# Moving the activation loads of the second half into buffers that the first half no longer needs

## The chip, the cores and the metric

The kernel runs on one core of one Trainium2 chip. The metric is device time in microseconds (us), median of several executions. "Span" is the length of one profiled execution; it is about 2 us shorter than the timed execution.

Short names: PE is the matrix engine (TensorE), PEld its loading of the operand that stays in place, DVE the vector engine, ACT the scalar engine, POOL the GpSimd engine. SPq is the queue of the sync engine, which issues nearly all loads. `ring` is a set of 20 buffers that all weights pass through, and the halo is the few columns of keys and values that a chunk takes over from the chunk before it. The granted clock is the share of full speed that TensorE was given. L552 means line 552 of that kernel's own source, so the same statement has different line numbers in different kernels.

## The reference, cut to what matters

```python
# S = 2048 rows, D = 1024, Df = 3584, 32 heads of 32, bf16
g = sigmoid((x * gate_w).sum(-1, keepdims=True))
# attention: every position looks at 8 positions, 2 apart, up to 14 back
qkv = x @ wqkv ; attn = softmax(q . k[pos - 2*w] * scale) ; a = (attn . v[pos - 2*w]) @ wo
# gated MLP
b = (gelu(x @ w_gate) * (x @ w_up)) @ w_down
out = g * a + (1 - g) * b
```

## The kernel before

The sequence is cut into four chunks of 512 rows. PE works in this order: transposes, QKV of chunks 0 and 1, gate/up pass of chunks 0 and 1, `down` of chunk 0, **QKV of chunks 2 and 3 together**, `down` of chunk 1, gate/up pass of chunks 2 and 3, `down` of chunks 2 and 3. The attention arithmetic of the chunks runs on DVE beside all this.

The larger products use seven half-size products in place of eight. This needs *forms*: sums and differences of quarters of the weights and of the activations. Most weight forms of `down` and gate/up are computed once and stored. The weight forms of the QKV product of chunks 2 and 3 are made by DVE just before use (L552, `ring<-ring`, 0.42 us each), and four activation forms (L449 to L454, `tf<-xr`, 1.2 us each) too.

Each engine runs its instructions in a fixed order. The Python program chooses this order at build time with a list scheduler: it keeps a modelled clock for every engine and always emits the operation that could start first by its own model.

```python
class Weave:
    def _emit(self, op, t):
        if op.eng in ("SP", "POOL"):            # a load: bytes at a modelled rate, issue cost
            nbytes, issue = op.cost
            self.clk[op.eng] = t + issue
            self.pipe = max(self.pipe, t) + nbytes / self.RATE
            op.end = self.pipe + 2.2
        else:
            self.clk[op.eng] = t + cost
        ...                                     # and is chained behind the engine's last instruction
    def run(self, streams):
        ...
                t = None if op is None else self._start(op)     # after all deps, by the model
                if t is not None and (best is None or t + s[0] < best[0]):
                    best = (t + s[0], t, s, op)
```

The parts that the change touches:

```python
xr = persist.tile([P, 4, KH, SC], BF16)                   # activations of two chunks
kT = [persist.tile([P, NT, HALO + SC], BF16, ...) for i in range(2)]   # keys: one per chunk parity
vT = [persist.tile([P, NT, HALO + SC], BF16, ...) for i in range(2)]   # values

def load_x(c, deps):                                      # 8 transposing loads of 128 KB a chunk
    for kt in range(KT):
        yield Op("SP", (P * SC * 2, 1.6), lambda kt=kt: nc.sync.dma_start_transpose(
            out=xT(c, kt), in_=x[c * SC:(c + 1) * SC, kt * P:(kt + 1) * P]), deps, key=("x", c, kt))

def loads():                                              # order of the load queue
    ...
    # among the weights of down(chunk 0): the 16 loads of chunks 2 and 3
    yield from load_down(c0, [o for c in (c0 + 2, c0 + 3) for o in load_x(c, [("ffn", sup)])])
    for which in range(3):
        yield from load_qkv(c0 + 2, which, ...)           # then the QKV weights
```

`xr` is read until the end of the first gate/up pass, so chunks 2 and 3 cannot be loaded earlier than that.

## Time and profile before

| what | value | view |
|---|---|---|
| time | 740.24 us (739.6 to 740.36, 3 runs) | timed runs |
| span | 738.2 us | page |
| PE busy | 723.9 us, 98% | page, part 1 |
| PE waiting for weight forms | 7.7 us in 3 pieces | waits |
| granted PE clock just after | 0.50, then 0.89 | windows |

The page's part 1 (busy time, share of the span, instructions):

```profile
PE 723.9 (98%) x3397; PEld 355.7 (48%) x3397; DVE 631.1 (85%) x935; ACT 312.7 (42%) x530; POOL 72.0 (10%) x128
```

Whom PE waited for, in the kernel before (us in total, times, longest):

```profile
PE ps L585 <- DVE ring L552: 7.7, 3, 4.2
PE ps L274 <- DVE hT L272: 1.2, 1, 1.2
PE ps L1191 <- DMA hT<-in_A_x_dram: 0.9, 1, 0.9
PE ps L1096 <- DMA ring<-in_A_wo_dram: 0.6, 2, 0.4
```

PE is the limit nearly everywhere. The only large wait is for L552, the QKV weight forms. The table of windows (each line: stretch in us, its length, then busy us of PE, PEld, DVE, ACT, POOL with instruction counts, granted clock, DMA share, GB/s) shows where it lies:

```profile
300.00:318.00 18.00, 17.35 (x79) 7.48 (x77) 17.86 (x22) 0.69 (x1) 2.69 (x5) 1.00 1.12 354
322.00:329.00 7.00, 0.81 (x2) 0.23 (x2) 7.00 (x13) 0.00 (x0) 0.00 (x0) 0.79 0.34 128
329.00:332.00 3.00, 2.55 (x7) 0.95 (x8) 3.00 (x11) 0.59 (x1) 0.00 (x0) 0.50 0.00 0
332.00:336.00 4.00, 4.00 (x18) 2.27 (x17) 3.30 (x10) 2.35 (x4) 0.00 (x0) 0.89 0.00 0
```

PE works 0.81 of 7 us at 322 to 329 us, and the clock falls to half within this stretch. Before that, DMA is saturated (share 1.12). The timeline of the load queue (start, duration, what was issued) shows the transposing loads standing in front of the QKV weights:

```profile
299.95 4.20 SPq L307 DMA_TRANSPOSE xr<-in_A_x_dram  x3
304.25 3.39 SPq L357 DMA_DIRECT2D ring<-dforms  x7
308.64 1.16 SPq L307 DMA_TRANSPOSE xr<-in_A_x_dram  x1
309.89 35.21 SPq L302 DMA_DIRECT2D ring<-in_A_wqkv_dram  x16
```

One more view belongs here, although the prediction made too little of it: DVE's timeline (start, duration, instruction, output<-input; an idle time before an instruction would stand in brackets at the end).

```profile
316.50 2.47 DVE L771 TENSOR_TENSOR xbuf<-xbuf 128x2048 bf16<-128x2048 bf16 x2
319.01 2.31 DVE L828 STREAM_TRANSPOSE xbuf<-xbuf 128x2048 bf16<-128x2048 bf16 x1
321.24 1.18 DVE L449 TENSOR_TENSOR tf<-xr 128x2048 bf16<-128x2048 bf16 x1
322.35 0.41 DVE L552 TENSOR_TENSOR ring<-ring 128x512 bf16<-128x512 bf16 x1
322.68 1.22 DVE L451 TENSOR_TENSOR tf<-xr,tf 128x2048 bf16<-128x2048 bf16 x1
...
328.98 4.78 DVE L552 TENSOR_TENSOR ring<-ring 128x512 bf16<-128x512 bf16 x14
```

No line has a bracket. The form at 322.35 was preceded by attention work of chunk 1 (L771, L828), with no idle time. So DVE was not waiting for weights when it reached the form. It was late by its own order. The landings say the same: the two loads that the first form needs were issued at 309.9 and 310.5 us and landed 4.9 and 5.1 us later, by 315.6 us, and the form came 6.8 us after that.

### The profile page before, as it was taken

How to read it: one execution, taken by the hardware profiler on the slowest of the kernel's cores; microseconds unless marked ns; L12 is line 12 of the kernel's file. 1: busy time of each engine (PE TensorE's matmuls, PEld its weight loads, DVE VectorE, ACT ScalarE, POOL GpSimd, SP SyncE). 2: the span in 40 equal slices, each digit the busy share in tenths (PEclk: the TensorE clock that was granted, in tenths of full speed). 3: DMA queues.
4: the chain of work that ended last, by engine and by line, in shares of the span. 5: the costliest groups of instructions: out<-in, count | busy, mean ns of one | idle time of the engine just before them, and what ended most of it. 6: DMA issues, size and time to landing. Idle time of an engine off the chain costs nothing.

```text
span 738.2 us, 9955 instructions
## 1 busy us (share of the span) xinstructions
PE 723.9 (98%) x3397; PEld 355.7 (48%) x3397; DVE 631.1 (85%) x935; ACT 312.7 (42%) x530; POOL 72.0 (10%) x128
## 2 busy tenths in 40 slices
PE   8999999999999999959999999999999999999997
PEld 5666644444444444425665444444444444444443
DVE  2689899999999999997999999989999999896300
ACT  2333455558555542015444122585558554310110
POOL 2235322121111000000000001000000000001000
PEclk9999999999999999989999999999999999999999
DMA  9999955555646469950235999746464545889993
GB/s 304 332 331 361 377 190 177 165 175 168 200 143 207 156 193 327 321 223 28 86 115 175 314 312 317 245 134 181 128 176 134 166 142 158 284 302 335 323 303 105
DMA packets 150435, 162.68 MB, mean 220 GB/s; under 512 B 22896, under 2 KB 110960, under 8 KB 150384
## 3 DMA queue, kind: packets, MB, share of 16 engines
q1 hardware_dynamic: 141552, 134.25, 59.0%
q0 software_dynamic: 8544, 27.27, 10.3%
q8 instruction: 26, 0.43, 0.2%
q10 hardware_dynamic: 288, 0.52, 0.2%
q14 instruction: 25, 0.20, 0.1%
HBM read 129.50 MB, written 28.31 MB: 214 GB/s over the span
## 4 chain that ended last, share of the span: by engine, by line
PE 95%; DMA 3%; DVE 1%; issue 0%; ACT 0%; DVEq 0%
PE ps L952 46%; PE ps L1096 28%; PE ps L469 11%; PE ps L585 10%; DMA ring<-in_A_wo_dram 1%; DMA ring<-oforms 1%; DMA ring<-in_A_wqkv_dram 1%; DMA hT<-in_A_x_dram 0%; PE ps L1191 0%; DVE zt L699 0%; DVE tf L451 0%; DVE tf L449 0%; PE ps L693 0%; DVE ring L552 0%; ACT ost L1131 0%
## 5 line engine op out<-in xcount | busy, mean ns | idle before, releaser
L952 PEld LDWEIGHTS <-ring 128*128 128x128 bf16 x1568 | 153.2, 98 | 185.0 <-issue 0.4
L952 PE MATMUL ps<-xr,ring 128*128 128x512 bf16 x896 | 212.3, 379 | 0.0
L952 PE MATMUL ps<-tf,ring 128*128 128x512 bf16 x672 | 164.0, 379 | 0.0
L1096 PE MATMUL ps<-ring,hT 128*128 128x512 bf16 x708 | 160.7, 379 | 0.0
L1096 PEld LDWEIGHTS <-hT 128*128 128x128 bf16 x708 | 69.2, 98 | 83.4
L765 DVE TENSOR_TENSOR xbuf<-qo,kT 128x2048 bf16<-128x2048 bf16 x64 | 77.5, 1218 | 2.1 <-ACT kT L491 2.1
L904 DVE TENSOR_TENSOR xbuf<-xbuf,vT 128x2048 bf16<-128x2048 bf16 x64 | 77.4, 1218 | 0.1
L771 DVE TENSOR_TENSOR xbuf<-xbuf 128x2048 bf16<-128x2048 bf16 x56 | 68.2, 1218 | 0.1
L585 PEld LDWEIGHTS <-ring 128*128 128x128 bf16 x336 | 44.0, 131 | 38.6 <-DVE ring L552 10.0
L1131 ACT ACTIVATE ost<-ps,omg 128x512 bf16<-128x512 f32 x16 | 11.0, 688 | 113.4 <-PE ps L1096 110.2
L469 PE MATMUL ps<-xr,ring 128*128 128x512 bf16 x256 | 56.1, 381 | 0.1
L981 ACT COPY ps<-ps 128x512 f32<-128x512 f32 x56 | 32.0, 571 | 55.0 <-PE ps L952 54.8
L1123 POOL DMA_DIRECT2D out_dram<-ost x24 | 13.0, 540 | 433.0 <-ACT ost L1131 339.2
L1024 ACT ACTIVATE gl<-ps 128x512 bf16<-128x512 f32 x56 | 33.5, 598 | 51.3 <-PE ps L952 50.9
L1096 PE MATMUL ps<-ring,qo 128*128 128x512 bf16 x192 | 49.6, 379 | 0.6 <-DMA ring<-in_A_wo_dram 0.6
L996 DVE TENSOR_TENSOR hT<-hT,gl 128x1024 bf16<-128x1024 bf16 x56 | 38.4, 686 | 8.6 <-ACT hT L993 7.6
L469 PEld LDWEIGHTS <-ring 128*128 128x128 bf16 x256 | 36.6, 144 | 19.0 <-issue 0.9
L585 PE MATMUL ps<-xr,ring 128*128 128x512 bf16 x192 | 43.5, 379 | 0.0
L1036 DVE TENSOR_TENSOR u<-ps,u 128x512 f32<-128x512 f32 x56 | 38.4, 686 | 5.3 <-PE ps L952 4.2
L585 PE MATMUL ps<-tf,ring 128*128 128x512 bf16 x144 | 35.1, 394 | 7.7 <-DVE ring L552 7.7
L912 DVE TENSOR_TENSOR xbuf<-xbuf 128x1024 bf16<-128x1024 bf16 x64 | 42.0, 686 | 0.6
L438 POOL DMA_DIRECT2D fforms<-ring x56 | 30.5, 544 | 119.3 <-DVE ring L430 115.4
(106 smaller groups left out, 728.1 us busy)
## 6 DMA issues: line engine op xcount, KB each, us to landing
ring<-dforms SPq DMA_DIRECT2D x112, 256.0 KB, 4.7
ring<-in_B_w_down_dram SPq DMA_DIRECT2D x84, 256.0 KB, 3.9
ring<-in_B_w_gate_dram SPq DMA_DIRECT2D x56, 256.0 KB, 4.8
fforms<-ring POOLq DMA_DIRECT2D x56, 256.0 KB, 4.4
ring<-fforms SPq DMA_DIRECT2D x56, 256.0 KB, 3.9
ring<-in_B_w_up_dram SPq DMA_DIRECT2D x42, 256.0 KB, 3.9
ring<-in_A_wqkv_dram SPq DMA_DIRECT2D x40, 256.0 KB, 5.7
ring<-oforms SPq DMA_DIRECT2D x32, 256.0 KB, 5.4
```

What stands on the lines that cost most here:

```text
L469: nc.tensor.matmul(banks[bk][:], lhsT=lhsT, rhs=xT(c, kt), start=(kt == 0), stop=(kt == KT - 1))
L585: nc.tensor.matmul(banks[bk][:], lhsT=lhsT, rhs=rhs[:, kt, :], start=(start and kt == 0), stop=(kt == KH - 1), skip_group_check=True)
L765: V(out=w3(box[t]), in0=q_b, in1=k_w, op=ALU.mult)
L771: V(out=w3(box[0]), in0=w3(box[0]), in1=w3(box[t]), op=ALU.add)
L904: return dve(tt(n), taking(("p", t), lambda: V(out=w3(box["p", t]), in0=w3(box["ab"]), in1=v_w, op=ALU.mult)), [("qkv", c, 2, t), abo] + ( ...
L912: V(out=s4(t)[:, t % 2], in0=w3(box["p", t])[:, 0:4], in1=w3(box["p", t])[:, 4:8], op=ALU.add)
L952: nc.tensor.matmul(banks[bk][:], lhsT=wv[:, k, fl * P:(fl + 1) * P], rhs=rhs[:, k, :], start=(start and k == 0), stop=(k == KH - 1), skip_ ...
L981: ev[f, "seed"] = act(0.5, lambda f=f: nc.scalar.copy(out=banks[Bk[f]][:], in_=banks[A[f]][:]), [o, fr] if fr else [o])
L996: yield dve(tt(2 * SC), lambda f=f: nc.vector.tensor_tensor(out=hT[:, :, f, :], in0=hT[:, :, f, :], in1=gl[f][:].rearrange("p (j s) -> p j ...
L1024: nc.scalar.activation(out=gl[f][:, SC:2 * SC], in_=banks[A[f]][:], func=ACT.Gelu_apprx_tanh)
L1036: e = dve(tt(SC, True), lambda f=f: nc.vector.tensor_tensor(out=u2[f][:], in0=banks[Dk[f]][:], in1=u2[f][:], op=ALU.add), [o, ev[f, "u2"]])
L1096: nc.tensor.matmul(banks[bk][:], lhsT=l, rhs=wv[:, i, :], start=(start and k == 0), stop=(q == last and i == 1), skip_group_check=True)
```

## The change

The intent: load the activations of chunks 2 and 3 during the first gate/up pass, where DMA has room, instead of while `down` of chunk 0 loads its weights. Room is found by letting them live in the key and value buffers of chunk 0, which are dead after chunk 0's attention, and by rotating six buffers among keys, values and activations. Chunk 3's values have no place yet when they are computed, so they wait in dead rows of `h` and are moved by DMA. Some smaller savings of memory come along: the halo is 14 instead of 16 columns, one gate buffer serves for three, and the gate's exponential is issued next to the softmax's. The core of the diff (cut):

```diff
-    xr = persist.tile([P, 4, KH, SC], BF16)
-    kT = [persist.tile([P, NT, HALO + SC], BF16, name=f"kT{i}") for i in range(2)]
-    vT = [persist.tile([P, NT, HALO + SC], BF16, name=f"vT{i}") for i in range(2)]
+    lend = [persist.tile([P, NT, HALO + SC], BF16, name=f"lend{i}") for i in range(6)]
+    xs = [z[:]... for z in lend[0:4]]                      # x of chunks 0..3
+    kT = [lend[2], lend[4], lend[0], lend[4]]
+    vT = [lend[3], lend[5], lend[1], lend[5]]
+    XB = 9
     def load_x(c, deps):
+        deps = deps + ([[("acct", 1)], [("att", 0)]][c - 2] if c > 1 else [])
@@ loads
         for b in range(2, NBLK):
             yield from load_block(0, b)
+            if b >= XB:                                    # after gate/up blocks 9, 10, 11, 12
+                for c, k0 in ((2, 0), (2, 4), (3, 0), (3, 4))[b - XB:b - XB + 1]:
+                    yield from list(load_x(c, []))[k0:k0 + 4]
-                yield from load_down(c0, [o for c in (c0 + 2, c0 + 3) for o in load_x(c, [("ffn", sup)])])
+                yield from load_down(c0)
@@ x_forms, of chunks 2 and 3
-            free = [("pr", c0 - 2, 2, 1), ("S2", c0 - 2, 0), ("S2", c0 - 2, 1)] if sup else []
+            free = [("ffn", sup - 1)] if sup else []
@@ qkv_pair: values of chunk 3
+            if odd and which == 2:
+                return v_tmp(t), ("v3", t), []             # dead h rows; v_move() copies them later
... (halo 14, scratch of down(0) in lend[0:2], merged exponentials, zq instead of zc and og)
```

More of the change, by code (lines that the diff above doesn't have):

```diff
@@ L18 @@
 DIL = 2
-HALO = 16
+HALO = 14
 SC = 512
@@ L192 @@
     qo = [persist.tile([P, NT, SC], BF16, name=f"qo{i}") for i in range(2)]
-    kT = [persist.tile([P, NT, HALO + SC], BF16, name=f"kT{i}") for i in range(2)]
-    vT = [persist.tile([P, NT, HALO + SC], BF16, name=f"vT{i}") for i in range(2)]
+    lend = [persist.tile([P, NT, HALO + SC], BF16, name=f"lend{i}") for i in range(6)]
+    xs = [z[:].rearrange("p t s -> p (t s)")[:, 0:NT * SC].rearrange("p (t s) -> p t s", s=SC) for z in lend[0:4]]
+    kT = [lend[2], lend[4], lend[0], lend[4]]
+    vT = [lend[3], lend[5], lend[1], lend[5]]
     NG = 20
@@ L207, in xT, with xq @@
     def xT(c, kt):
-        return xr[:, 2 * (c % 2) + kt // KH, kt % KH, :]
+        return xs[c][:, kt, :]
+    def xq(c, hi):
+        return xs[c][:, KH * hi:KH * (hi + 1), :]
     def hflat(j, f0, n):
@@ L339, with load_down @@
     SEQ = [("A11", "B11"), ("A12", "B21"), ("S1", "T1"), ("S2", "T2"), ("S3", "T3"), ("S4", "B22"), ("A22", "T4")]
-    def load_down(c, extra=(), first=()):
-        extra = list(extra)
+    def load_down(c, first=()):
         for m, (_, name) in enumerate(SEQ):
@@ L359, in load_down @@
                     ([("stored", "o" if o else "d")] if name[0] == "T" else []) + [("w", 0, NBLK - 1, 3)] + list(first))
-            if m >= 1:
-                yield from extra[:3]
-                extra = extra[3:]
     def loads():
@@ L389, in loads @@
                                         [("wq", c0 + 2, which - 1, 3, KH - 1)] if which else [])
-                yield from load_down(c0 + 1, (), [("wq", c0 + 2, 2, 3, KH - 1)])
+                yield from load_down(c0 + 1, [("wq", c0 + 2, 2, 3, KH - 1)])
                 for b in range(NBLK):
@@ L442, in x_forms @@
     def x_forms():
-        b12, b22, b11, b21 = xr[:, 0], xr[:, 1], xr[:, 2], xr[:, 3]
         t = tt(KH * SC)
@@ L447, in x_forms @@
             dx = [("x", c0 + 1, kt) for kt in range(KT)]
-            free = [("pr", c0 - 2, 2, 1), ("S2", c0 - 2, 0), ("S2", c0 - 2, 1)] if sup else []
-            t1 = dve(t, lambda: V(out=tf[:, 0], in0=b12, in1=b11, op=ALU.subtract), dx + free, lag=1.0, key=("xf", sup, 1))
+            b12, b22, b11, b21 = xq(c0, 0), xq(c0, 1), xq(c0 + 1, 0), xq(c0 + 1, 1)
+            free = [("ffn", sup - 1)] if sup else []
+            t1 = dve(t, lambda b12=b12, b11=b11: V(out=tf[:, 0], in0=b12, in1=b11, op=ALU.subtract), dx + free, lag=1.0, key=("xf", sup, 1))
             yield t1
-            t2 = dve(t, lambda: V(out=tf[:, 1], in0=b22, in1=tf[:, 0], op=ALU.subtract), [t1], key=("xf", sup, 2))
+            t2 = dve(t, lambda b22=b22: V(out=tf[:, 1], in0=b22, in1=tf[:, 0], op=ALU.subtract), [t1], key=("xf", sup, 2))
             yield t2
-            yield dve(t, lambda: V(out=b12, in0=b22, in1=b12, op=ALU.subtract), [("z", c0)], key=("xf", sup, 3))
-            yield dve(t, lambda: V(out=tf[:, 2], in0=b21, in1=tf[:, 1], op=ALU.subtract), [t2], key=("xf", sup))
+            yield dve(t, lambda b12=b12, b22=b22: V(out=b12, in0=b22, in1=b12, op=ALU.subtract), [("z", c0)], key=("xf", sup, 3))
+            yield dve(t, lambda b21=b21: V(out=tf[:, 2], in0=b21, in1=tf[:, 1], op=ALU.subtract), [t2], key=("xf", sup))
     gates = {}
     def qkv_dst(c, which, t):
-        cc = c % 2
-        return (qo[cc][:, t, :], kT[cc][:, t, HALO:HALO + SC], vT[cc][:, t, HALO:HALO + SC])[which]
+        return (qo[c % 2][:, t, :], kT[c][:, t, HALO:HALO + SC], vT[c][:, t, HALO:HALO + SC])[which]
     def qkv_w(c, which, kt):
@@ L471, in halo @@
     def halo(c):
-        cc, pc = c % 2, 1 - c % 2
         for z, n in ((kT, 1), (vT, 2)):
-            yield act(0.2, lambda z=z: nc.scalar.copy(out=z[cc][:, :, 0:HALO], in_=z[pc][:, :, SC:SC + HALO]),
-                      [("qkv", c - 1, n, t) for t in range(NT)] + ([("acct", 2 * c - 3), ("att", c - 2)] if c > 2 else []),
+            src = [("qkv", c - 1, n, t) for t in range(NT)]
+            yield act(0.2, lambda z=z: nc.scalar.copy(out=z[c][:, :, 0:HALO], in_=z[c - 1][:, :, SC:SC + HALO]),
+                      src + ([("acct", 2 * c - 3), ("att", c - 2)] if c > 2 else []),
                       key=("halo", c, n))
@@ L562, in q_tmp, with v_tmp, v_move, fn @@
         return hT[:, t // 2, FT - NT + KH * (t % 2):FT - NT + KH * (t % 2 + 1), :].rearrange("p f s -> p (f s)")
+    def v_tmp(t):
+        v = hT[:, t, FH:FH + KH, :] if t < 2 else hT[:, 2 + (t - 2) // 3, NTH + KH * ((t - 2) % 3):NTH + KH * ((t - 2) % 3 + 1), :]
+        return v.rearrange("p f s -> p (f s)")
+    def v_move(c):
+        deps = [("v3", t) for t in range(NT)] + [("att", c - 2)]
+        dst = vT[c][:, :, HALO:HALO + SC]
+        def fn():
+            nc.sync.dma_start(out=dst[:, 0:2], in_=hT[:, 0:2, FH:FH + KH, :].rearrange("p j f s -> p j (f s)"))
+            for j in range(2):
+                nc.sync.dma_start(out=dst[:, 2 + 3 * j:5 + 3 * j],
+                                  in_=hT[:, 2 + j, NTH:NTH + 3 * KH, :].rearrange("p (u f) s -> p u (f s)", f=KH))
+        o = Op("SP", (P * NT * SC * 2, 1.5), fn, deps)
+        yield o
+        for t in range(NT):
+            w.done["qkv", c, 2, t] = o
     def qkv_pair(c):
-        T3, B22, B11, B21 = xr[:, 0], xr[:, 1], xr[:, 2], xr[:, 3]
+        T3, B22, B11, B21 = xq(c, 0), xq(c, 1), xq(c + 1, 0), xq(c + 1, 1)
         T1, T2, T4 = tf[:, 0], tf[:, 1], tf[:, 2]
@@ L571, in dst @@
                 return q_tmp(t), ("q3", t), []
-            d = [[], [("acct", 2 * c - 1)], [("att", c - 1)]][which] if odd else []
+            if odd and which == 2:
+                return v_tmp(t), ("v3", t), []
+            d = [("acct", 2 * c - 1)] if odd and which else []
             return qkv_dst(c + odd, which, t), ("qkv", c + odd, which, t), d
@@ L705, in gate @@
         yield e
-        zc = small.tile([P, SC // 32], F32, tag="zc", bufs=2, name="zc")
         ez = small.tile([P, SC // 32], F32, tag="ez", bufs=2, name="ez")
         omg = small.tile([P, NST], F32, tag="omg", bufs=3, name="omg")
-        gates[c] = (ez, omg, zc, zq)
+        gates[c] = (ez, omg, zq)
     def gate_sum(c):
         i, free = bank_take()
-        zc, zq = gates[c][2:]
+        zq = gates[c][2]
         def go():
@@ L720, in gate_sum @@
         yield o
-        e = dve(0.1, lambda: nc.vector.tensor_scalar(out=zc[:], in0=banks[i][:, 0:SC // 32], scalar1=ZMAX, scalar2=-ZMAX,
+        e = dve(0.1, lambda: nc.vector.tensor_scalar(out=zq[:], in0=banks[i][:, 0:SC // 32], scalar1=ZMAX, scalar2=-ZMAX,
                                                      op0=ALU.min, op1=ALU.max), [o], key=("zc", c))
@@ L724, in gate_sum @@
         bank_give(i, e)
-    def gate_exp(c):
-        ez, zc = gates[c][0], gates[c][2]
-        e = act(0.1, lambda: nc.scalar.activation(out=ez[:], in_=zc[:], func=ACT.Exp), [("zc", c)], table="exp", lag=1.0,
-                key=("ez", c))
-        yield e
     def gate_tail(c):
-        ez, omg = gates[c][:2]
+        ez, omg, og = gates[c]
         def tail():
-            og = small.tile([P, SC // 32], F32, tag="og", name="og")
             nc.vector.tensor_scalar(out=og[:], in0=ez[:], scalar1=1.0, scalar2=1.0, op0=ALU.mult, op1=ALU.add)
@@ L751, in scores @@
         for c in range(NCH):
-            q_, k_ = qo[c % 2], kT[c % 2]
+            q_, k_ = qo[c % 2], kT[c]
             for a in range(SC // AC):
@@ L803, in att_half @@
         a0 = a * AC
-        q_, v_ = qo[c % 2], vT[c % 2]
+        q_, v_ = qo[c % 2], vT[c]
         box = {}
@@ L860, in att_half, with exps @@
         yield o
-        if a == 0:
-            yield from gate_exp(c)
-        e = act(0.55, lambda: nc.scalar.activation(out=lsb(), in_=lsb(), func=ACT.Exp, scale=scale), [o], table="exp",
-                lag=0.6)
+        def exps():
+            if a == 0:
+                nc.scalar.activation(out=gates[c][0][:], in_=gates[c][2][:], func=ACT.Exp)
+            nc.scalar.activation(out=lsb(), in_=lsb(), func=ACT.Exp, scale=scale)
+        e = act(0.65 if a == 0 else 0.55, exps, [o] + ([("zc", c)] if a == 0 else []), table="exp", lag=0.6,
+                key=("ez", c) if a == 0 else None)
         yield e
@@ L945, in ffn @@
     def ffn(sup, mid, early=()):
-        T3, B22, B11, B21 = xr[:, 0], xr[:, 1], xr[:, 2], xr[:, 3]
+        T3, B22, B11, B21 = xq(2 * sup, 0), xq(2 * sup, 1), xq(2 * sup + 1, 0), xq(2 * sup + 1, 1)
         T1, T2, T4 = tf[:, 0], tf[:, 1], tf[:, 2]
@@ L1051, in down @@
             S1h, S1o = hT[:, 0:2, 0:FH, :], hT[:, 2:4, 0:NTH, :]
+        elif c + 1 < NCH:
+            S1h, S1o = [z[:].rearrange("p t s -> p (t s)")[:, 0:2 * n * P].rearrange("p (g f s) -> p g f s", g=2, f=n)
+                        for z, n in ((lend[0], FH), (lend[1], NTH))]
         else:
@@ L1193, in main @@
                 yield o
-                dst = xr[:, k0 // KH, :, j * P:(j + 1) * P]
+                dst = xs[0][:, k0:k0 + KH, j * P:(j + 1) * P]
                 if ne % 2:
@@ L1226, in main @@
                 yield from halo(c0 + 3)
+            if more:
+                yield from v_move(c0 + 3)
             for part in down(c0 + 1):
```

## The prediction

> **What bounds the kernel now.** The matrix engine (PE): busy 723.9 of 738.2 us on the page, and 95% of the chain of waits. By the list of who waited for whom, PE waits 7.7 us, in three pieces, for weight forms that the vector engine (DVE) makes for the second QKV projection, 0.6 us for `wo` weights, and some 2 us at the start. The timeline puts the 7.7 us at 321 to 329 us. DVE is busy over 94% in most stretches, but off the chain elsewhere.
>
> **Why PE waits there.** While `down` of chunk 0 runs (260 to 318 us), the load queue mixes 16 transposing loads of chunks 2 and 3 with the `down` weights: about 1.25 us of the queue each, a plain 256 KB load 0.48. By the table of stretches DMA is at its ceiling there (354 GB/s at 300 to 318 us), but at a share of 0.54 to 0.59 in the first gate/up pass. So the QKV weights are issued only from 309.9 us on, and DVE then has forms, gate transposes and four activation forms (1.2 us each) to do at once. After the gap the granted clock is 0.50 (329 to 332 us) and 0.89 (332 to 336): about 1.9 us more. The Trainium skill, "TensorE: Matmul & The Clock Gate", Part 1, says that an idle window of about 3.4 us halves the clock; this trace agrees.
>
> **What the change does.** The transposes move to the first gate/up pass, two activation forms ahead of the QKV stage. By the static order DVE's first weight form comes right after the last evacuation of `down`, ahead of most of chunk 1's last scores, not after them. Removed: 7.7 + 1.9 + 0.6 = 10.2 us, all on the chain. The matmul count is unchanged (3397), so the floor is about 730 us.
>
> **What it adds.** (a) The load queue must wait until chunk 0's attention ends before it loads chunk 3, with block 12's weights behind. That attention ended at 229 us; the new order ends it before the 21st h product, near 223. Transposes 5 us, loads landing in 4 to 5: block 12 near 234, needed near 236. Stall 0 to 3 us. (b) Chunk 3's values take a detour of 1 MB (the similar q move took 9.4 us), needed tens of us later: nothing. (c) Two more table loads (1.28 us each) on ACT, 42% busy. (d) PE reaches `down` of chunk 1 10 us sooner, near 392 us; chunk 1's attention ends near 393, needed by 395: 0 to 2 us. (e) Halo 14 keeps the 4-byte alignment: same durations.
>
> **Prediction.** 740.2 - 10.2 + 1.5 = 731.5 us, range 729 to 737. Faster by over 2%: 0.04; within 2%: 0.93; slower: 0.03.
>
> **What the profile should show.** PE waits for weight forms near 0, clock 1.0 in the QKV stage; QKV weights issued at 301 to 308 us; PE there 10 us earlier, and the lead kept to the end; DMA share of the first pass near 0.65 after 150 us; matmul spacing unchanged.
>
> **What would make it wrong.** Block 12's weights late, PE idle near 236 us for over 3 us and a slow clock after it; QKV weights still late because ring slots, not the transposes, hold them; DVE's new order stalling before an evacuation, which moves the wait to later QKV groups or to chunk 1's `down`.

## The result, and the profile after

The changed kernel gives correct results. Its median is 731.4 us (731.03 to 732.67, 4 runs); the kernel before had 739.92 us (739.6 to 740.36, 4 runs) on the same chip. The ratio is 0.9887, 95% interval 0.987 to 0.9905. All ratios here are the mean time of one kernel's fast runs over that of the other's fast runs in the same rounds, so they are not quite the ratio of the quoted medians.

Page, part 1, and the waits of PE, after:

```profile
PE 721.8 (99%) x3397; PEld 356.0 (49%) x3397; DVE 631.6 (87%) x935; ACT 314.9 (43%) x532; POOL 72.0 (10%) x128
```

```profile
PE ps L970 <- ACT m L1024: 2.1, 1, 2.1
PE ps L279 <- DVE hT L277: 1.2, 1, 1.2
PE ps L1212 <- DMA hT<-in_A_x_dram: 0.8, 1, 0.8
```

The wait for weight forms is gone and a new one of 2.1 us has come. The windows of the QKV stage after:

```profile
300.00:318.00 18.00, 18.00 (x96) 7.97 (x94) 17.82 (x30) 1.43 (x3) 2.16 (x4) 1.00 0.83 291
322.00:329.00 7.00, 7.00 (x35) 4.24 (x33) 6.54 (x10) 2.83 (x5) 0.00 (x0) 1.00 0.00 0
329.00:332.00 3.00, 3.00 (x15) 1.97 (x14) 3.00 (x4) 1.74 (x3) 0.00 (x0) 1.00 0.00 0
332.00:336.00 4.00, 4.00 (x20) 2.25 (x19) 3.93 (x3) 2.68 (x5) 0.00 (x0) 1.00 0.33 107
```

PE is busy throughout, at full clock. The load queue after, and DVE's timeline around the first forms (the form is L556 here):

```profile
212.38 6.73 SPq L313 DMA_TRANSPOSE lend<-in_A_x_dram  x4
...
301.88 42.01 SPq L307 DMA_DIRECT2D ring<-in_A_wqkv_dram  x22
```

```profile
309.83 0.75 DVE L1191 SCALAR_TENSOR_TENSOR ost<-ps,omg,u2d 128x512 bf16<-128x512 f32 x1
310.49 0.42 DVE L556 TENSOR_TENSOR ring<-ring 128x512 bf16<-128x512 bf16 x1
...
314.90 3.44 DVE L556 TENSOR_TENSOR ring<-ring 128x512 bf16<-128x512 bf16 x10
...
331.69 2.48 DVE L787 TENSOR_TENSOR xbuf<-xbuf 128x2048 bf16<-128x2048 bf16 x2
334.20 2.31 DVE L844 STREAM_TRANSPOSE xbuf<-xbuf 128x2048 bf16<-128x2048 bf16 x1
```

Two things have changed at once. The QKV weights are issued 8.0 us earlier (301.88 against 309.89). And DVE's *order* is different: the forms now stand ahead of the rest of chunk 1's scores and of their transpose (L787 and L844 here, L771 and L828 before), which come 15 us later. Two of the four activation forms have also moved away, to 271.9 and 283.7 us. The two traces alone do not say which of the two brought the gain.

The lead of PE over the kernel before, by the timelines: 0.9 us at the start of the QKV stage, 10.8 us at the start of `down` of chunk 1 (391.05 against 401.86) and at the start of the second gate/up pass, 8.5 us in the span. The lost 2.3 us are mostly the new wait of 2.1 us in that pass.

### The profile page after: what moved, and what is told of

Same layout as the page of the kernel before. It is cut to its first block, busy times and chain, and to the rows that moved or that the text cites. A ratio compares the mean times of both kernels' runs of the same rounds, so it can differ in the third digit from the quotient of the medians.

```text
span 729.7 us, 9971 instructions
## 1 busy us (share of the span) xinstructions
PE 721.8 (99%) x3397; PEld 356.0 (49%) x3397; DVE 631.6 (87%) x935; ACT 314.9 (43%) x532; POOL 72.0 (10%) x128
## 4 chain that ended last, share of the span: by engine, by line
PE 73%; issue 21%; DVE 2%; ACT 1%; DMA 1%; POOL 1%; POOLq 0%; ACTq 0%
PE ps L970 44%; PE ps L1117 17%; PE ps L473 11%; DVE xbuf L922 1%; POOL out_dram L1144 1%; DMA hT<-in_A_x_dram 0%; DVE xbuf L930 0%; PE ps L1212 0%; DMA out_dram<-ost 0%; DVE xbuf L935 0%; DVE ost L1191 0%; ACT ost L1152 0%; ACT L1058 0%; DVE xbuf L787 0%; PE ps L717 0%
## 5 line engine op out<-in xcount | busy, mean ns | idle before, releaser
L970 PE MATMUL ps<-lend,ring 128*128 128x512 bf16 x896 | 212.3, 379 | 2.2 <-ACT m L1024 2.1
L970 PE MATMUL ps<-tf,ring 128*128 128x512 bf16 x672 | 164.0, 379 | 0.0
L781 DVE TENSOR_TENSOR xbuf<-qo,lend 128x2048 bf16<-128x2048 bf16 x64 | 77.4, 1218 | 2.1 <-ACT lend L495 2.1
L922 DVE TENSOR_TENSOR xbuf<-xbuf,lend 128x2048 bf16<-128x2048 bf16 x64 | 77.4, 1218 | 0.1
L787 DVE TENSOR_TENSOR xbuf<-xbuf 128x2048 bf16<-128x2048 bf16 x56 | 68.2, 1218 | 0.2
L473 PE MATMUL ps<-lend,ring 128*128 128x512 bf16 x256 | 56.3, 381 | 0.1
L609 PE MATMUL ps<-lend,ring 128*128 128x512 bf16 x192 | 43.5, 379 | 0.0
L1033 DVE TENSOR_TENSOR hT<-ps,m 128x512 bf16<-128x512 f32 x56 | 38.4, 686 | 4.0 <-PE ps L970 3.9
```

Of the source, the lines that this page charges most:

```text
L473: nc.tensor.matmul(banks[bk][:], lhsT=lhsT, rhs=xT(c, kt), start=(kt == 0), stop=(kt == KT - 1))
L609: nc.tensor.matmul(banks[bk][:], lhsT=lhsT, rhs=rhs[:, kt, :], start=(start and kt == 0), stop=(kt == KH - 1), skip_group_check=True)
L781: V(out=w3(box[t]), in0=q_b, in1=k_w, op=ALU.mult)
L787: V(out=w3(box[0]), in0=w3(box[0]), in1=w3(box[t]), op=ALU.add)
L922: return dve(tt(n), taking(("p", t), lambda: V(out=w3(box["p", t]), in0=w3(box["ab"]), in1=v_w, op=ALU.mult)), [("qkv", c, 2, t), abo] + ( ...
L970: nc.tensor.matmul(banks[bk][:], lhsT=wv[:, k, fl * P:(fl + 1) * P], rhs=rhs[:, k, :], start=(start and k == 0), stop=(k == KH - 1), skip_ ...
```

## The experiments

Twelve kernels were run, in three batches. "Before" in the same batches measured 739.97, 740.01 and 740.77 us.

**1. Loads back in their old place.** Everything of the change is kept (buffers, detour of the values, halo, exponentials); only the place of the 16 loads is undone.

```diff
-            if b >= XB:  (the 16 loads after blocks 9..12)
-                yield from load_down(c0)
+                yield from load_down(c0, (), [o for c in (c0 + 2, c0 + 3) for o in load_x(c, [("ffn", sup)])])
```

> The changed kernel with only the timing of the 16 transposing loads undone: they are issued among the down weights of chunk 0 again, buffers, halo and merged gate exponential kept. My theory (the gain comes from taking these loads out of that stream): 738 to 742 us, PE waits 6 to 10 us for weight forms near 320 us again, and the granted clock falls there. Rival (buffers, merged exponential or the rebuilt static order bring the gain): 730 to 733 us.

Measured: 739.76 us, ratio 0.9997 (0.9985 to 1.0009). PE waits again:

```profile
PE ps L610 <- DVE ring L557: 7.6, 3, 3.8
```

So all of the gain hangs on where the loads stand, and the value detour, the halo and the table loads cost nothing, on balance, that shows. But the scheduler gives this kernel another DVE order, with late forms. The experiment cannot say whether the transfers or the order matter.

**2. All activation forms in the QKV stage.** The changed kernel, with its activation forms made only there. Orders of PE, ACT and loads are those of the changed kernel.

```diff
-            free = [("ffn", sup - 1)] if sup else []
+            free = [("ffn", sup - 1), ("z", c0)] if sup else []
```

> The changed kernel, loads early, but the four activation forms of the second half are held until the gate matmul of chunk 2, as late as before. Theory that late weights caused the gap: 732 to 733.5 us, PE waits 1 to 2 us for the first activation form. Rival, that the pile-up of activation forms on DVE caused it: 736 us or more, a wait of over 4 us at 320 us and a lowered clock after it.

Measured: 732.21 us, ratio 0.9898 (0.9883 to 0.9912), with one new PE wait of 1.2 us, for an activation form. The times do not resolve it (the changed kernel has 0.9887, and 0.989 in the control below), so the early activation forms are a minor part at most.

**3. Late weights with the new order.** The changed kernel, with 16 tiny copies between DRAM tensors in the load queue ahead of the QKV weights. The scheduler counts them as free, so PE, DVE and ACT keep exactly the order of the changed kernel.

```diff
                 yield from load_down(c0)
+                yield Op("SP", (0, 0.0), lambda: [nc.sync.dma_start(out=sdram[i], in_=x[i * P:(i + 1) * P, 0:64])
+                                                  for i in range(16)])
```

> The changed kernel with 16 tiny copies (16 KB each, between tensors in DRAM, read by nobody) in the load queue just before the QKV weights, so that these are issued about 8 us later, near 310 us as before; all other orders are the same. Theory that late weights caused the gap: 733 to 737 us, DVE idle 3 to 6 us ahead of the first weight form, PE then waits 2 to 5 us at 325 to 330 us. Rival (activation forms): 731 to 732 us.

Measured: 737.16 us, ratio 0.9965 (0.9951 to 0.9978). The weights were issued at 313.31, even later than in the kernel before. Here PE waits for the weights themselves, and DVE stands idle before the forms:

```profile
PE ps L612 <- DMA ring<-in_A_wqkv_dram: 2.6, 3, 0.9
PE ps L612 <- DVE qo L673: 1.6, 1, 1.6
```

```profile
317.36 0.43 DVE L559 TENSOR_TENSOR ring<-ring 128x512 bf16<-128x512 bf16 x1 [6.30 <-issue]
320.62 0.42 DVE L559 TENSOR_TENSOR ring<-ring 128x512 bf16<-128x512 bf16 x1 [1.70 <-DMA ring<-in_A_wqkv_dram]
```

With the new order, late weights do cost: some 5.8 us (737.16 against 731.4, of another batch) for 11.4 us of lateness. Even so this kernel is 2.8 us faster than the one before, whose weights were issued 3.4 us sooner. The time lies just outside the expected 733 to 737 us.

**4. The scalar engine's table loads and the new wait.** The first theory for the new 2.1 us wait was the two added table loads on ACT, so the softmax exponential was allowed in a gate/up pass only right after one certain copy.

```diff
-        yield e
+        yield lambda: e if not w.ffn_on or w.act_kind == "m5" or w.table == "exp" else None
```

> The changed kernel with each softmax exponential inside a gate/up pass issued on ACT right after the m5 copy, not between the u2 copy and the seed copy. Theory that the new 2.1 us wait of PE for the m5 copy near 565 us comes from the two table loads (1.28 us each) landing at a bad place in ACT's sequence: 729 to 729.8 us, no wait of PE for ACT. Rival (ACT has simply too much to do in that period, 3.3 us more): the wait stays, 731 to 732 us.

Measured: 732.41 us, ratio 0.9899 (0.9885 to 0.9912). The wait of 2.1 us stayed. This theory fell. The waits view gives no times, and I had put the wait near 565 us; PE's timeline shows it at 454 to 456 us:

```profile
456.32 1.89 PE L970 MATMUL ps<-lend,ring 128*128 128x512 bf16 x8 [2.07 <-ACT m L1024]
```

There ACT itself had waited 3.76 us for DVE's sum `u` (its activation at 455.16 us), and DVE reached that sum only after chunk 2's attention, again with no idle time before it:

```profile
453.31 1.22 DVE L922 TENSOR_TENSOR xbuf<-xbuf,lend 128x2048 bf16<-128x2048 bf16 x1
454.44 0.69 DVE L1054 TENSOR_TENSOR u<-ps,u 128x512 f32<-128x512 f32 x1
```

**5. The cost of the cold clock.** The kernel before, with 30 dummy matmuls into a spare bank, put into the gap.

```diff
+                if which == 0 and g == 0:
+                    for i in range(30):
+                        nc.tensor.matmul(banks[wb][:], lhsT=B11[:, 0, 0:P], rhs=B11[:, i % KH, :], start=True, stop=True)
```

> The kernel before, with 30 dummy matmuls (about 6.5 us of TensorE work into a spare bank) put between the first two QKV products and the two that wait for the late weight forms, near 320 us. The orders of the vector, scalar and DMA queues are those of before. Theory: of the 8.5 to 8.8 us that the change gains, about 2.2 us are not waiting but slow clock after TensorE had stood nearly idle for some 8 us; so with dummies in that gap the forms come just as late, the granted clock stays near 1.0 from 322 to 336 us (before: 0.79, 0.50, 0.89), and the time falls by 1.5 to 2.5 us to about 738. Rival: the slow clock costs nothing beyond the wait, or the dummies delay the next products; then 739.5 to 741.

Measured: 738.68 us, ratio 0.9978 (0.9965 to 0.9992); the clock is 1.00 from 318 to 350 us. PE starts the bulk of the products that need the forms at 329.53 (before: 329.45), but runs them at full speed. So some 1.6 us (0.22% of 740; by the interval 0.6 to 2.6) of the loss before were slow clock, not waiting. The trace before fits this as an estimate: PE worked at half clock from 329.45 to about 332.9 us, which costs half of 3.4 us.

**6. The same loads on another queue.** The kernel before, with the loads of chunks 2 and 3 issued from ACT's queue.

```diff
+        q = nc.scalar if c > 1 else nc.sync
-            yield Op("SP", (P * SC * 2, 1.6), lambda kt=kt: nc.sync.dma_start_transpose(
+            yield Op("SP", (P * SC * 2, 0.0 if c > 1 else 1.6), lambda kt=kt: q.dma_start_transpose(
```

> The kernel before, with the transposing loads of chunks 2 and 3 at the same place in the program but issued from the scalar engine's DMA queue instead of the one that issues the weights. It tells two reasons for the late QKV weights apart. Queue theory: the weights stood behind the transposes in one queue (265 to 309 us); freed of them they are issued about 302 to 308 us as in the changed kernel, and most of the gap at 322 to 329 us goes: 731 to 735 us. Bandwidth theory: the 16 DMA engines were full there and the transposes take their time wherever they are issued, so that the weights land as late as before and the time stays at 738 to 741 us, with three waits of the TensorE for the forms as in the kernel before.

Measured: 751.79 us, ratio 1.0152 (1.0126 to 1.0177), worse than either theory. The QKV weights were issued at 311.7 us, no earlier, although no transpose stood in their queue. The `down` weights now came late, and the orders of DVE and ACT had changed as well, with a PE wait of 5.6 us for `vT` later on. The Trainium skill, "DMA: Bandwidth & Descriptors", section "Issuing engines are not separate DMA queues", says that loads of several issuing engines run on the same 16 DMA engines and interleave; this run agrees: from 255 to 335 us the packets of the two queues took 68.0% and 19.8% of the 16 engines' time for 19.14 MB, and those of the one queue before 80.4% for the same bytes, so a queue of their own freed no engine time. PE waited 3.5 us for `down` forms in DMA, which it had not done before. But it is not a clean test: weights need free ring slots, which come only as PE goes on with `down`, and PE itself was late here. And it cannot say whether late weights were the reason for late forms.

**7. The first sum of the second pass moved up.** The changed kernel; the scheduler holds attention back by 3 us while it places the first block of the second gate/up pass. By the built program the orders of PE's work and of the load queue are the same. DVE's, by the traces, starts to differ at the first `u`: four attention instructions (3.5 us) come after it instead of before it (the expectation counts five, 4.0 us). Contrary to the expectation, the order also differs later, at 179 of DVE's 935 places up to 637 us and at 31 of ACT's.

```diff
+                bias = s[0] + (self.hold if s[0] >= 0.3 else 0.0)
-                if t is not None and (best is None or t + s[0] < best[0]):
-                    best = (t + s[0], t, s, op)
+                if t is not None and (best is None or t + bias < best[0]):
+                    best = (t + bias, t, s, op)
@@ ffn
+            w.hold = 3.0 if sup and i < 1 else 0.0
```

> The changed kernel; only the vector engine's order at the start of the second gate/up pass differs: five instructions of chunk 2's attention (4.0 us) come after the first sum u of the pass instead of before it (and the scalar engine's next exp after the second gelu). TensorE and load orders are the same. Theory: the 2.1 us wait of TensorE for m at 456 us is the vector engine's fixed order meeting a TensorE that now arrives 10.8 us earlier; with u moved ahead the wait goes and the time is 729.0 to 730.0 us, 1.4 to 2.4 us less than the changed kernel. Rival (the wait comes from the scalar engine's table loads or from elsewhere): the wait stays or moves on by a few us, and the time is 731 to 732.5 us.

Measured: **728.26 us** (727.65 to 728.44, 4 runs), ratio to before 0.9837 (0.9822 to 0.9851). No wait in the second pass is left in the list of PE's waits (its first two lines), and DVE's timeline has the sum at 450.41 us instead of 454.44:

```profile
PE ps L281 <- DVE hT L279: 1.2, 1, 1.2
PE ps L1215 <- DMA hT<-in_A_x_dram: 0.6, 1, 0.6
```

```profile
450.41 0.68 DVE L1057 TENSOR_TENSOR u<-ps,u 128x512 f32<-128x512 f32 x1
```

This version beats both kernels. PE had no other wait in this pass, so the later differences of order had no wait there to remove. The gain is larger than the 2.1 us of the wait. Against the control of the same batch it is 3.9 us (mean 728.16 against 732.10 us). In that control's timeline PE loses, beyond 0.216 us for each matmul, 2.23 us at the wait and 0.94, 0.42 and 0.33 us in the next 8 us, 3.9 us together; the version here loses none of it. The second part is a lowered clock after the wait (windows of the control):

```profile
457.00:459.00 2.00, 1.79 (x5) 0.70 (x5) 1.97 (x4) 1.14 (x3) 0.00 (x0) 0.58 1.05 318
```

In the profile of the changed kernel from its first batch the same wait of 2.07 us left the clock at 1.00. So this wait costs 2.1 us in some executions and nearly 4 in others. That the profile and the means both give 3.9 us is partly chance, because the profiled control is its slowest execution (734.11 us).

**8. Control.** The changed kernel once more.

> The changed kernel once more, as the control on this chip: 731.4 us, with one wait of 2.1 us of TensorE for m near 456 us and the granted clock at 1.0 throughout 318 to 350 us.

Measured: 732.25 us (730.58 to 734.11, 5 runs), ratio 0.989 (0.9872 to 0.9908), with the wait of 2.1 us again.

**9. No loads at all, old order.** The kernel before without the 16 transfers. Its output is wrong, which doesn't matter for the time. PE, DVE and ACT keep exactly the order of the kernel before, because the scheduler still counts the loads.

```diff
-  lambda kt=kt: nc.sync.dma_start_transpose(
+  lambda kt=kt: None if c > 1 else nc.sync.dma_start_transpose(
```

> Wrong on purpose: the kernel before without the 16 transposing loads of chunks 2 and 3 (the old contents of the buffer are used). The orders of TensorE, vector and scalar engine are exactly those of before; only those 16 transfers are missing. It gives the most that moving the loads can bring where they stood. Theory (transfer time of the DMA engines in the stage of the first down product): QKV weights issued 302 us or a little earlier instead of 309.9, the three waits for weight forms (9 to 15 us on the list, 8.8 of lost time) gone, and 730 to 733 us. If the time is far below 731, the changed kernel still pays for the loads elsewhere; if it is over 736, the loads weren't what made the weights late.

Measured: 740.57 us, ratio 0.9993 (0.998 to 1.0005). **No gain**, although the QKV weights were issued as early as in the changed kernel. The load queue, PE's waits and DVE's order (three views of this run):

```profile
302.01 17.17 SPq L302 DMA_DIRECT2D ring<-in_A_wqkv_dram  x14
```

```profile
PE ps L585 <- DVE ring L552: 8.6, 3, 3.9
```

```profile
319.50 2.31 DVE L828 STREAM_TRANSPOSE xbuf<-xbuf 128x2048 bf16<-128x2048 bf16 x1
321.73 1.18 DVE L449 TENSOR_TENSOR tf<-xr 128x2048 bf16<-128x2048 bf16 x1
322.83 0.41 DVE L552 TENSOR_TENSOR ring<-ring 128x512 bf16<-128x512 bf16 x1
```

The first form comes at 322.83, against 322.35 before, while its weights were issued from 302.01 on and landed in 4.6 us (median). DVE's order holds the forms back, not the weights. My expectation of 730 to 733 us was wrong.

**10. Plain loads instead of transposing ones.** Also with the orders of the kernel before. Its output is wrong, which doesn't matter for the time.

```diff
-  nc.sync.dma_start_transpose(out=xT(c, kt), in_=x[c * SC:(c + 1) * SC, kt * P:(kt + 1) * P])
+  nc.sync.dma_start(out=xT(c, kt), in_=x[c * SC + kt * 64:c * SC + (kt + 1) * 64, :].rearrange("a (b s) -> (a b) s", b=2))
```

> Wrong on purpose: as the kernel before, with the 16 transposing loads of chunks 2 and 3 replaced at the same place by plain copies of the same number of bytes (rows of 1 KB). Tells whether the bytes or the transposing cost the time. In the run with the loads on the scalar queue 2.1 MB of transposes took 15.8 us of all 16 engines, against 6.7 us for the same bytes of weights. If it is the transposing: the weights are issued 4 to 6 us earlier than in before, and the time is 733 to 736 us. If it is the bytes alone: as before, 739 to 741 us. If even a queue with plain loads lets the forms come in time: 731 to 733 us.

Measured: 739.98 us, ratio 0.9989 (0.9976 to 1.0001), PE waits 8.4 us for forms. The weights were issued at 305.11 us. So of the 7.9 us by which the 16 loads delayed the weights (309.89 against 302.01 in experiment 9), 4.8 us come from transposing and 3.1 us from the bytes and their issue. But as in experiment 9, none of this reaches the time under the old order. The time matches the "bytes alone" expectation, and read without experiment 9 it would have led to a wrong conclusion.

**11 and 12. How exact must the place be?** The version of experiment 7 with the loads after gate/up blocks 10 to 13, and after blocks 7 to 10, instead of 9 to 12 (`XB = 10`, `XB = 7`). Both also get another DVE order, from 216 and from 168 us on.

> The faster version (sum u earlier) with the loads of chunks 2 and 3 one gate/up block later, after blocks 10 to 13, so that the last four transposes stand just ahead of the first weights of the down product. Theory: the place has slack of several us, because the DMA engines are about a quarter idle in this pass and four transposes need about 4 us; 728 to 729.5 us, no new wait of TensorE over 1 us. Rival: the last group delays the first down weights, a wait of 1 to 4 us near 250 us, and 730 to 733 us.

Measured: 728.54 us, ratio 0.9836 (0.9821 to 0.9851), no new wait. One block later is free, with the order that the scheduler makes for it.

> The faster version with the loads two blocks earlier, after blocks 7 to 10, so before chunk 0's attention has let go of its keys and values (about 223 us). Theory: the transposes into those buffers hold up the one load queue until the attention lets go; gate/up weights behind them come late, and TensorE waits 2 to 10 us for weights between 190 and 230 us: 731 to 740 us. Rival: enough weights are loaded ahead and the time stays within 1 us of the faster version (727.5 to 729.5). Its vector order also differs in that pass.

Measured: 744.52 us, ratio 1.0058 (1.0042 to 1.0073). Two blocks earlier costs more than the whole change brings. One PE wait, the load queue and DVE's timeline show why (L437 makes the weight forms of a gate/up block):

```profile
PE ps L972 <- DVE ring L437: 13.9, 1, 13.9
```

```profile
197.57 1.07 SPq L344 DMA_DIRECT2D ring<-in_B_w_up_dram  x2
198.75 1.00 SPq L344 DMA_DIRECT2D ring<-in_B_w_gate_dram  x2
```

```profile
225.33 1.22 DVE L783 TENSOR_TENSOR xbuf<-qo,lend 128x2048 bf16<-128x2048 bf16 x1
226.46 2.61 DVE L437 TENSOR_TENSOR ring<-ring 128x1024 bf16<-128x1024 bf16 x4
```

The load queue does stand still for 14.6 us on attention work of DVE, in front of a transpose, up to 189.3 us, and the weights of block 10 behind it are issued late. But they had all landed by 203.8 us, and PE stood from 213 to 227 us for their forms, which DVE made only at 226.46 us, after attention and with no idle time before it. So this wait too is DVE's order, as in the kernel before, and not the queue directly. The scheduler's log of this build has these weights issued at 223.8 us and their first form at 228.6; the chip issued them at 197.6.

### What the experiments say together

Four kernels form a square of the two suspects:

| | QKV weights issued at 302 us | issued late |
|---|---|---|
| DVE's order of before (forms after the scores) | 740.57 (experiment 9) | 740.0 (before; 309.9 us) |
| DVE's order of after (forms before them) | 731.4 (after) | 737.16 (experiment 3; 313.3 us) |

Early weights are worth nothing under the old order. Under the new order they are needed. The kernel with the new order is 2.8 us faster than the one before even with weights later than ever, though not by the order alone: it keeps the two early activation forms and reaches the QKV stage 0.4 us sooner. The whole gain needs both.

Why does moving 16 loads change DVE's order? Because the scheduler chooses it by its own model of the loads. Its log (a property of the build, not a time on a chip, and found again in a second build) places the last transposing load of the kernel before at 316.4 us, landing at 322.3, and the QKV weights at 318.0 us, landing from 323.0 on; the chip issued those weights at 309.9. So the model saw free DVE time until 323 us and filled it with scores. In the changed kernel it has the weights land from 309.7 us on, and puts the first form at 312.4 us. The change worked through a build-time model that was 8 us late for this stage.

What stays open: the new order with the weights issued at exactly 309.9 us was not run. As an estimate from experiment 3, if each us of lateness between 309.9 and 313.3 us cost one us, that kernel would take about 733.8 us (737.16 - 3.4); at the average of experiment 3, half a us for each, about 735.5 us. Half of the gain or more would be order. The split of the gain at that point is not measured.

## Why the prediction was right or wrong, point by point

- **The time.** 731.5 us (729 to 737) was predicted and 731.4 measured. That they agree to 0.1 us is partly luck: PE won 10.8 us and not 10.2, and lost 2.3 and not 1.5, at a place that was not named; and the control measured 732.25. The gain was foreseen by reading the new static order as built; the reason given for it was only half of it (third point).
- **What bounds the kernel, and where the gap is.** Right: all of the 7.7 us for forms went, and the clock stayed at 1.00. The slow clock was put at 1.9 us and measured 1.6 us (0.6 to 2.6) in experiment 5.
- **Why PE waits.** This step was right as a description and wrong as a cause: "So the QKV weights are issued only from 309.9 us on, and DVE then has forms [...] to do at once." The weights were late, but experiment 9 issued them at 302 us and gained nothing. The binding cause was DVE's fixed order. The prediction did see the order change ("ahead of most of chunk 1's last scores, not after them"), but took it as a side effect; experiments 3 and 9 show that it is a necessary half. The hint was in the profile of before: DVE had no idle time ahead of the form. I did not see it there before experiment 9, from which I still expected 730 to 733 us.
- **The removed time, 10.2 us.** PE's lead at `down` of chunk 1 was 10.8 us. Right within 0.6 us.
- **(a) Stall of 0 to 3 us on chunk 0's attention.** There was no stall: the last group of transposes was issued at 212.4 us and the next weights at 222.3 us, in time. In experiment 12 the queue did stall there, for 14.6 us, but the 13.9 us that PE lost came from DVE's order.
- **(b), (c), and the halo.** Nothing was expected of the detour, the halo and the table loads, and experiments 1 and 4 show nothing.
- **(d) 0 to 2 us at `down` of chunk 1.** The size was right (2.1 us), the place was not: it came 63 us later, at the start of the second gate/up pass. The reason is of the kind foreseen among the risks: DVE's order meeting a PE that arrives 10.8 us earlier. So "the lead kept to the end" was wrong by 2.3 us (10.8 to 8.5).
- **Signs.** QKV weights at 301.9 us (301 to 308 predicted); DMA share 0.77 at 150 to 200 us and 0.67 at 200 to 250 us (0.65 predicted, too low in the first).

The rule of the clock came from the Trainium skill, "TensorE: Matmul & The Clock Gate", Part 1, "What's actually happening", which gives an idle window of about 3.4 us after which TensorE runs at half its clock. The trace before (0.50 at 329 to 332 us after 7 us with 0.81 us of work) and experiment 5 (1.00 with dummies) agree that little work lowers the clock. They do not show that 3.4 us without any work are needed: see the last section.

## What to carry to other kernels

When PE waits for a producer, look at the idle time in front of the *producer*. If it has none, its inputs are not what holds it there; its place in its own engine's order is, and faster loads under that order will bring nothing. Experiments 9 and 12 both show it. In a kernel whose order is fixed at build time, moving a load changes the order of other engines too, so separate the two with a build that keeps the order and drops the transfer, and one that keeps the order and delays it. And after such a gain, look at the next places where the now earlier engine meets an unchanged order: there, one sum placed ahead of 3.5 us of attention took away a wait of 2.1 us and, with the slow clock after it, brought 3.9 us on the mean.

## What the Trainium skill lacked or had wrong

- "Perfetto Trace Analysis", "Optimization Strategy": it says to find the gaps of the limiting engine and the semaphore that it waits on, and to make that dependency start sooner or complete faster. It lacks the step of asking whether the producer itself was waiting. Here the form had no idle time in front of it, and removing 16 loads ahead of its weights moved 740.0 to 740.57 us.
- No page that I used says that a kernel's build-time model of load times decides the order of the compute engines, and that a wrong model costs time: weights modelled at 318.0 us were issued at 309.9 us, and under the order built on that the first form came at 322.35 us, though its weights had landed by 315.6.
- "DMA: Bandwidth & Descriptors", "Latency and other measured facts", gives a transposing load 261 GB/s, or 350 to 400 GB/s when contiguous. In experiment 6, where the transposes have a queue of their own, 2.10 MB took 19.8% of the 16 engines' time in 80 us, which is 133 GB/s; the weights beside them took 68.0% for 17.04 MB, 313 GB/s. Both were measured with DMA nearly saturated, so the ratio of 2.4 says more than either number.
- "TensorE: Matmul & The Clock Gate", Part 1, speaks of an idle window of about 3.4 us. Less was enough here. In the kernel before the clock fell at 326.1 us, 0.8 us after the last matmul; no gap until then was over 1.9 us, and PE had worked 0.81 of the last 3.4 us. In experiment 3 it fell at 322.4 us, after gaps of 0.76, 0.94 and 0.91 us with PE busy 0.96 of the last 3.4 us. And one gap of 2.07 us in otherwise unbroken work lowered it to 0.50 for about 3.4 us in the profiles of experiments 2, 4 and 8, but not in those of the changed kernel and of experiment 3. So PE need not be idle for 3.4 us; how much work keeps the clock up is not settled. The page has something like it only under "A second HAM failure mode", for short pauses between matmul groups, without a figure for how much work keeps the clock up.
